# A first layer's last block in two phases: its second product by Strassen's scheme

## The chip, the cores and the metric

The kernel runs on one core of one Trainium2 chip. The metric is the device time of the program in microseconds (us), the median of several executions; lower is better. One execution of each kernel is taken with the hardware profiler, and all views below come from that one. Engines: PE is TensorE (matmuls), DVE is VectorE, ACT is ScalarE, POOL is GpSimd, SP is SyncE. In this kernel SP and POOL mostly issue DMA transfers, each in the order of its own queue: SP mainly loads, POOL mainly stores.

## What is computed

A linear attention with decay, then two MLPs, all in float32 (the weights are drawn in float64 and come to the chip as 64-bit words):

```python
for t in range(S):                                   # 768 steps, 4 batches, 8 heads, D = 64
    state = gamma * state + einsum('bhd,bhe->bhde', k[:, :, t], v[:, :, t])
    y[:, :, t] = scale * einsum('bhd,bhde->bhe', q[:, :, t], state)
x = y.transpose(0, 2, 1, 3).reshape(3072, 512)
h = x @ w_in;   x = np.maximum(0.01 * h, h) @ w_out          # 512 -> 2048 -> 512
h = np.maximum(x @ w_in2, 0.0);   out = (h * h) @ w_out2     # 512 -> 2048 -> 512
```

## The kernel before

**Precision.** Each float32 operand is split into a high and a low part (ACT rounds a copy, DVE subtracts it), and each product is three matmuls: high by high, low by high, high by low. A matmul here has a 128x128 stationary tile and 512 moving columns.

**Blocks.** The 3072 tokens go in three blocks b of 1024. The 2048 hidden rows are 8 pairs q of 128-row tiles. The work on PE stands in this order: block 0 of the first layer, with the attention for it and for block 1 between its matmuls, then blocks 1 and 2 of the first layer, then the three blocks of the second. All matmuls and DMA issues are pinned in the order in which the code is written; on ACT and DVE a scheduler places the rest. Blocks are named (layer, b): (0, 2) is the first layer's last, and the one that is changed.

**First product.** In block 0 it is plain (`emit_plain`). From block 1 on it is a Strassen-Winograd scheme: the 2x2 quarters of the weights and of x give seven products in place of eight. The seven weight sums, split, are tiles `wa` (four units) and `wb` (three), kept in DRAM as `wid`; the seven x sums are made by `operands`.

**Second product, first layer.** Plain in all three blocks. Per block there are two halves of 512 tokens. The first half's matmuls (`put_out`) stand between those of the first product of the following q; the second half (`emit_out` with t = 1) runs after the last q. Each half is 16 tiles of 12 matmuls. The weights are tiles `wo`, loaded from DRAM (`wou`, four raw units for each q) by `read_out`; `make_out` makes them in block 0.

**Second layer, `both_block`.** Two phases. The first is all of the first product, 42 matmuls for each q; its results `gu` and `gt` stay in SBUF. `first_half` does the first four products of q, while `second_half` of q - 1 does its last three, so PE turns to the next q's units after four products. The second phase is the second product as seven Strassen stages of 48 matmuls: `prepare` makes the next stage's g operand (`rot`) during a stage, and the weights `wu` come from `wou` with eight units for each q, four raw and four sums, loaded by `read_stage`.

**Weights.** `cast` makes float32 of float64 words: two passes on ACT, three on DVE. The second layer's `w2` is cast in pieces during the first two blocks (`SOON`; tiles `st` and `sf`, stored as `wflt`). For q in `HERE`, 0 to 4, its second half is loaded and cast in block (0, 2) as one tile `sg` (`units_ahead`), split and summed (`make_units`, `out_units`) and stored to `wou`.

Of the kernel before, what the change touches and what calls it, by code (L numbers as in the profile page):

```python
# [17 lines left out]
P = 128  # L18
# [7 lines left out]
T = 512  # L26
# [17 lines left out]
HERE = (0, 1, 2, 3, 4)  # L44
# [9 lines left out]
def retention_then_two_mlps(  # L54
# [12 lines left out]
    mid = ExitStack()  # L67
    w_p = mid.enter_context(tc.tile_pool(name="w", bufs=1))
# [10 lines left out]
    def swap_pools():  # L79
        early.close()  # L80
        late["ps"] = ctx.enter_context(tc.tile_pool(name="ps_b", bufs=1, space=bass.MemoryType.PSUM))
        late["p"] = mid.enter_context(tc.tile_pool(name="late", bufs=1, reuse_waits="tile"))

    def swap_left():
        mid.close()
        late["p"] = ctx.enter_context(tc.tile_pool(name="units", bufs=1, reuse_waits="tile"))
# [250 lines left out]
    wou = [dram.tile([P, 8 if lay else 4, NQ, 2, 256], F32, name=f"wou{lay}") for lay in range(2)]  # L337
# [16 lines left out]
    def load_piece(n):  # L354
        if n < 2 * len(SOON):
# [40 lines left out]
    def in_tiles(b, q):  # L396
        if b == 1 and q % 2 == 0:
            return [w_p.tile([P, 512 * n], F32R, tag="sg", name=t, bufs=2) for n, t in ((4, "wa"), (3, "wb"))]
        pool = late["p"] if q % 2 and late else w_p
        return [pool.tile([P, 512 * n], F32R, tag=t, name=t, bufs=1) for n, t in ((4, "wa"), (3, "wb"))]  # L400
# [150 lines left out]
    def get_in(b, q):  # L551
        if b == 0:
            plain_in(q)
        else:
            read_wid(0, q, *in_tiles(b, q))

    def make_out(q):
        if q < NQ - 1:
            f = g_p.tile([P, 2, T], F32, tag=f"t{NQ - 1}", name="of", bufs=1).rearrange("p j c -> p (j c)")
        else:  # L560
            f = w_p.tile([P, 1024], F32, tag="wf", name="of", bufs=1)
# [3 lines left out]
        put_wou(q, o)  # L565

    def put_wou(q, o):
        store(
            out=wou[0][:, :, q].rearrange("p n l c -> p n (l c)"),
            in_=o.bitcast(F32).rearrange("p n l c -> p n (l c)"),  # L570
        )
        wout[q] = (o[:, 0:2], o[:, 2:4])

    def out_units(q, n, h, t):
# [4 lines left out]
            out=wou[1][:, n:2 + n, q].rearrange("p n l c -> p n (l c)"),  # L579
# [3 lines left out]
    def make_units(q, f, *to):  # L583

        if q in HERE:
            t = late["p"].tile([P, 1024], U64, tag="sg", name="sg")
            store(out=t, in_=w2[q, 1])
            yield
            cast(t, f)
        else:  # L590
            store(out=f, in_=wflt[q, 1])
        yield
        h = [f[:, n * 512:n * 512 + 512].rearrange("p (n c) -> p n c", n=2) for n in range(2)]
        for n in range(2):
            out_units(q, 2 * n, h[n], to[n])
        yield
# [6 lines left out]
        for n in range(2):  # L603
            out_units(q, 4 + 2 * n, h[n], to[2 + n])

    def scratch(*tags):
        out = []
        for t in tags:
            p = late["r"] if t == "ss" else g_p if t[0] == "t" else late["p"]
# [3 lines left out]
    def read_out(q, spare=None):  # L613
        if spare == "u":
            o = [late["p"].tile([P, 2, 2, 256], F32R, tag=f"u{n}", name="wo", bufs=1) for n in range(2)]
            for n in range(2):
                load(
                    out=o[n].bitcast(F32).rearrange("p n l c -> p n (l c)"),
                    in_=wou[0][:, 2 * n:2 * n + 2, q].rearrange("p n l c -> p n (l c)"),
                )  # L620
        else:
            p, tag, bufs = spare or (o_p, "wo", 2)
            t = p.tile([P, 4, 2, 256], F32R, tag=tag, name="wo", bufs=bufs)
            load(
                out=t.bitcast(F32).rearrange("p n l c -> p n (l c)"),
                in_=wou[0][:, :, q].rearrange("p n l c -> p n (l c)"),
            )
            o = (t[:, 0:2], t[:, 2:4])
        wout[q] = o
# [55 lines left out]
    def act_sbuf(g, on_act):  # L685
        if on_act:
# [99 lines left out]
    def evacuate(b, t):  # L786
        ac = acc.pop((0, b, t))
        for m in range(KB):
            if t:
                if m % 2 == 0:  # L790
# [490 lines left out]
```

## Time and profile before

| | us |
|---|---|
| median of 3 executions | 1108.33 (1108.21 to 1111.32) |
| the profiled execution | 1108.09 |
| its span (first to last instruction) | 1106.3 |
| PE busy | 1094.2 (99% of the span) |
| DVE busy | 703.6 (64%) |
| ACT busy | 582.0 (53%) |
| moved by DMA | 283.87 MB, mean 257 GB/s |

The profile's page gives busy times; its chain of waits follows the work that ended last back through what released it; its tables of stretches give each engine's busy time between two moments. "PEclk" is the clock that the chip granted to PE, 1.00 being full speed. An idle engine costs time only if PE waits for it in the end.

### The profile page before, as it was taken

What the parts mean: (1) busy time and instruction counts of PE and PEld (TensorE: products, weight loads), DVE (VectorE), ACT (ScalarE), POOL (GpSimd) and SP (SyncE); (2) the same over time, 40 slices, a digit from 0 to 9 for tenths busy, and PEclk for the clock granted to TensorE, in tenths of its full rate; (3) what the DMA queues carried; (4) which work ended last, traced back from release to release, by engine and by line L of the source; (5) the groups of instructions that cost most, each with busy time, mean ns of one, the idle gap of its engine ahead of it and who ended that gap; (6) DMA issues with size and microseconds to landing.
All of it is one profiled execution on the core that took longest, in us unless ns stands there. A gap on an engine that the chain in (4) does not pass through costs nothing.

```text
span 1106.3 us, 15285 instructions
## 1 busy us (share of the span) xinstructions
PE 1094.2 (99%) x5647; PEld 869.0 (79%) x5647; DVE 703.6 (64%) x1205; ACT 582.0 (53%) x1052; POOL 77.6 (7%) x134
## 2 busy tenths in 40 slices
PE   9999999999999999999999999999999999999998
PEld 6777777677777777788787788888888888888886
DVE  5867776656666564545448548886655768455853
ACT  5666665444564552355456357655455555455542
POOL 0000000001000000001111112100000001000000
PEclk9999999999999999999999999999999999999999
DMA  9688885867689876599985877989155875357571
GB/s 372 226 307 303 304 312 163 315 199 280 228 300 344 323 225 224 170 347 327 336 322 195 325 255 270 383 284 360 64 177 185 319 250 233 124 194 251 167 244 58
DMA packets 81227, 283.87 MB, mean 257 GB/s; under 512 B 7808, under 2 KB 10368, under 8 KB 72960
## 3 DMA queue, kind: packets, MB, share of 16 engines
q1 hardware_dynamic: 64208, 210.33, 54.8%
q0 software_dynamic: 16800, 72.36, 16.8%
q8 instruction: 45, 0.74, 0.3%
q10 hardware_dynamic: 144, 0.20, 0.1%
q14 instruction: 30, 0.25, 0.1%
HBM read 205.79 MB, written 77.07 MB: 256 GB/s over the span
## 4 chain that ended last, share of the span: by engine, by line
PE 82%; issue 8%; DMA 5%; DVE 3%; POOL 1%; ACT 1%; SPq 0%; POOLq 0%; DVEq 0%; ACTq 0%
PE acc L127 38%; PE pa L127 23%; PE pd L127 8%; PE y L127 5%; PE pb L127 4%; PE sc L127 3%; DMA r<-first 3%; DMA wo<-wou 1%; DMA wflt<-sf 1%; POOL wou L133 1%; PE idle L127 1%; DMA wou<-of 0%; DMA wf<-wraw 0%; DVE gl L763 0%; DVE of L389 0%
## 5 line engine op out<-in xcount | busy, mean ns | idle before, releaser
L127 PE MATMUL acc<-rot,wu 128*128 128x512 f32 x1008 | 235.7, 395 | 0.0
L127 PEld LDWEIGHTS acc<-rot,wu 128*128 128x128 f32 x1008 | 189.2, 188 | 46.0
L127 PE MATMUL pa<-xh,wa 128*128 128x512 f32 x576 | 180.9, 395 | 0.1
L127 PE MATMUL acc<-gh,wo 128*128 128x512 f32 x600 | 160.3, 399 | 3.3 <-DMA wo<-wou 2.5
L127 PEld LDWEIGHTS acc<-gh,wo 128*128 128x128 f32 x600 | 112.4, 190 | 31.5 <-issue 4.6
L127 PEld LDWEIGHTS pa<-xh,wa 128*128 128x128 f32 x576 | 106.1, 188 | 25.4 <-issue 2.2
L127 PE MATMUL pa<-xl,wa 128*128 128x512 f32 x288 | 112.5, 391 | 0.0
L837 ACT CAST rot<-gu 128x512 fp32r<-128x512 f32 x120 | 74.5, 621 | 61.6 <-PE acc L127 54.4
L838 DVE TENSOR_TENSOR rot<-gu,rot 128x512 fp32r<-128x512 f32 x120 | 82.1, 689 | 38.5 <-ACT rot L837 38.0
L127 PE MATMUL pd<-xh,wa 128*128 128x512 f32 x320 | 99.2, 390 | 1.3 <-DVE wa L485 0.7
L127 PE MATMUL pa<-xh,wb 128*128 128x512 f32 x320 | 99.8, 393 | 0.0
L127 PE MATMUL acc<-gl,wo 128*128 128x512 f32 x300 | 85.4, 392 | 0.0
L763 DVE TENSOR_TENSOR gl<-g,gh 128x512 fp32r<-128x512 f32 x75 | 50.6, 687 | 35.0 <-ACT gh L762 20.1
L127 PEld LDWEIGHTS pd<-xh,wa 128*128 128x128 f32 x320 | 60.0, 188 | 15.2 <-DVE wa L485 1.4
L127 PEld LDWEIGHTS pa<-xh,wb 128*128 128x128 f32 x320 | 59.5, 188 | 12.9
L127 PEld LDWEIGHTS acc<-gl,wo 128*128 128x128 f32 x300 | 56.3, 188 | 12.9 <-DVE gl L763 0.3
L127 PEld LDWEIGHTS pa<-xl,wa 128*128 128x128 f32 x288 | 54.1, 188 | 11.6
L127 PE MATMUL acc<-gg,wo 128*128 128x512 f32 x252 | 62.9, 398 | 0.0
L127 PE MATMUL pa<-xl,wb 128*128 128x512 f32 x160 | 62.4, 390 | 0.0
L127 PE MATMUL pd<-xl,wa 128*128 128x512 f32 x160 | 62.4, 390 | 0.0
L127 PEld LDWEIGHTS acc<-gg,wo 128*128 128x128 f32 x252 | 46.8, 188 | 11.9 <-issue 1.4
L687 ACT ACTIVATE gt<-gt 128x512 f32<-128x512 f32 x48 | 30.4, 633 | 46.6 <-DVE gt L856 32.5
(141 smaller groups left out, 1628.3 us busy)
## 6 DMA issues: line engine op xcount, KB each, us to landing
wu<-wou SPq DMA_DIRECT2D x84, 512.0 KB, 5.5
wo<-wou SPq DMA_DIRECT2D x32, 1024.0 KB, 8.2
wa<-wid SPq DMA_DIRECT2D x28, 1024.0 KB, 7.4
wb<-wid SPq DMA_DIRECT2D x28, 768.0 KB, 5.3
sg<-w SPq DMA_DIRECT2D x16, 1024.0 KB, 7.4
wou<-of POOLq DMA_DIRECT2D x32, 512.0 KB, 5.8
r<-first SPq DMA_DIRECT2D x50, 256.0 KB, 6.9
wid<-wa POOLq DMA_DIRECT2D x12, 1024.0 KB, 7.1
```

Of the source, the lines that this page charges most:

```text
L127: pin(nc.tensor.matmul(**kw))
L133: pin(nc.gpsimd.dma_start(**io))
L687: nc.scalar.activation(out=g, in_=g, func=AF.Relu)
L763: mark[1] = seq(nc.vector.tensor_tensor(out=gl, in0=g, in1=gh.bitcast(F32), op=ALU.subtract)).ins
L837: mark[0] = nc.scalar.copy(r[:, 0], s).ins
L838: mark[1] = nc.vector.tensor_tensor(out=r[:, 1], in0=s, in1=r[:, 0].bitcast(F32), op=ALU.subtract).ins
```

## The change

- Block (0, 2) is run by `both_block` as well, with `lay` 0: first product for all q, then the second product in seven stages.
- `wou` of the first layer gets eight units for each q. The four sums are made and stored in block 0 by `out_sums`, behind `make_out` of the next q.
- `HERE` is 0 to 3. Their units are made in the first phase of (0, 2) by `units_inline`, which loads the float64 words in two halves `st` from POOL's queue; q = 4 is cast in block (0, 1) by `last_pieces`, and its units are made in the second phase.
- `gu` tiles lie where weight tiles lay (`kept`); the pools are swapped in block (0, 1), not after (0, 2). The load of `xs` for (1, 0) moves from the first product of (0, 2) into its fourth stage; `units_here` of q = 0 and 1 moves into the second phase.
- `make_in(1, 0)` and its loads move from the end of block 0's first half into its second half.

```diff
-HERE = (0, 1, 2, 3, 4)
+HERE = (0, 1, 2, 3)
...
-    wou = [dram.tile([P, 8 if lay else 4, NQ, 2, 256], F32, name=f"wou{lay}") for lay in range(2)]
+    wou = [dram.tile([P, 8, NQ, 2, 256], F32, name=f"wou{lay}") for lay in range(2)]
...
+    def out_sums(q):
+
+        with aside():
+            to = [x_p.tile([P, 2 * T], F32, tag=t, name="of") for t in ("xh4", "xl4")]
+            sum_units(0, q, stage.pop(("of", q)), *to)
...
+    def units_inline():
+
+        def get(q):
+            kinds = ((late["r"], "ss", 2), (w_p, "wf" if q < 2 else "wb", 1))
+            t = [p.tile([P, 512], U64, tag=tag, name="st", bufs=n) for p, tag, n in kinds]
+            for n in range(2):
+                store(out=t[n], in_=w2[q, 1][:, 512 * n:512 * n + 512])
+            return t
+
+        st = get(HERE[0])
+        yield
+        to = quarters()
+        for q in HERE:
+            f = late["r"].tile([P, 1024], F32, tag="ss", name="of", bufs=2)
+            for n in range(2):
+                cast(st[n], f[:, 512 * n:512 * n + 512])
+            if q + 1 in HERE:
+                st = get(q + 1)
+            yield
+            yield from all_units(q, f, *to)
+            yield
+        f = x_p.tile([P, 1024], F32, tag="xl4", name="of")
+        yield from make_units(HERE[-1] + 1, f, *to)
...
+    def kept(q):
+
+        if q in (5, 7):
+            return w_p.tile([P, 2, T], F32, tag="wf" if q == 5 else "wb", name="gu", bufs=1)
+        if q not in ahead:
+            t = w_p.tile([P, 2, 2, T], F32, tag="wa" if q == 4 else "sg", name="gu", bufs=1 if q == 4 else 2)
+            ahead[q], ahead[6 if q == 4 else q + 1] = t[:, 0], t[:, 1]
+        return ahead.pop(q)
...
+                if lay == 0 and n and (k == 1 or k == 3 and n in (1, 2, 4, 5)):
+                    with aside():
+                        next(here, None)
...
+        at = {4: (7, 13), 5: (5, 11), 6: (1, 5, 9)} if lay else {4: (13,), 5: (5, 11), 6: (1, 4, 8, 12)}
...
-                    if n == 1 and not last:
-                        read_x(b + 1)
-                    if n in (3, 5) and not last:
-                        read_units((n - 3) // 2)
...
+                    if n == (1 if lay else 3) and nl is not None:
+                        read_x(nb)
+                    if n in (3, 5) and lay and nl is not None:
+                        read_units(1, (n - 3) // 2)
+                if lay == 0:
+                    if (n, e) in ((0, 1), (0, 9), (0, 15)):
+                        with aside():
+                            next(here, None)
+                    if (n, e) in ((1, 1), (2, 13)):
+                        made = units_here(n - 1, x_p.tile([P, 1024], F32, tag="xh4", name="of"))
+                        next(made)
...
+                    if q:
+                        plain_in(q + 1)
+                        for n in (q - 1,) if q < 5 else (4, 5) if q == 5 else (6,):
+                            out_sums(n)
...
+            if b == 0 and i in (2, 11):
+                load_in(i // 11)
+            elif b == 0 and i == 6:
+                with aside():
+                    for _ in make_in(1, 0):
+                        pass
...
+            elif b == 1 and i == 12:
+                swap_left()
+                swap_right()
+                here = units_inline()
+                next(here)
+                read_units(0, 1)
...
+    for lay, b in ((0, NB - 1), (1, 0), (1, 1), (1, 2)):
+        both_block(lay, b, here)
```

Where the instructions stand is shown at three places. The first is DVE in a q-step of block 0, the step that the timeline of the rows below shows (`pm` and `s` belong to the attention, `wf` is the next q's first weights, `sf` a piece of `w2`, `of` the second weights of the first layer). Before:

```order
L388 TENSOR_SCALAR wf<-wf 128x1024
L389 SCALAR_TENSOR_TENSOR wf<-sg,wf 128x1024
L763 TENSOR_TENSOR gl<-g,gh 128x512
L392 ISA wf<-sg,wf 128x2048
L233 TENSOR_TENSOR pm<-sc,tab_79 128x256 x2
L241 SCALAR_TENSOR_TENSOR s_1394<-state,tab_78,sc 128x64
L388 TENSOR_SCALAR sf<-sf 128x512
L389 SCALAR_TENSOR_TENSOR sf<-st,sf 128x512
L392 ISA sf<-st,sf 128x1024
L419 TENSOR_TENSOR wa<-wf,wa 128x1024
```

The same step of the changed kernel:

```order
L578 TENSOR_TENSOR of<-of 128x256
L384 SCALAR_TENSOR_TENSOR wf<-sg,wf 128x1024
L579 TENSOR_TENSOR of<-of 128x256
L387 ISA wf<-sg,wf 128x2048
L580 TENSOR_TENSOR of<-of 128x256
L228 TENSOR_TENSOR pm<-sc,tab_79 128x256 x2
L236 SCALAR_TENSOR_TENSOR s_1430<-state,tab_78,sc 128x64
L383 TENSOR_SCALAR sf<-sf 128x512
L581 TENSOR_TENSOR of<-of 128x256
L384 SCALAR_TENSOR_TENSOR sf<-st,sf 128x512
L387 ISA sf<-st,sf 128x1024
L413 TENSOR_TENSOR wa<-wf,wa 128x1024
```

Four additions (`of<-of 128x256`) came in: two inside the conversion of `wf`, one behind it, one between `pm` and `wa`.

The second is ACT in the first product of (0, 2). Before, `g` rows bring PE's results out, and the cast of a whole `sg` tile stands in one place between two q:

```order
L720 ACTIVATE g<-pa 128x512
L762 CAST gh<-g 128x512 x2
L386 ACTIVATE of<-sg 128x1024
L387 ACTIVATE sg<-sg 128x1024
L682 COPY g<-pa 128x512
L682 COPY g<-pd 128x512
L576 CAST of<-of 128x2x256 x2
L682 COPY g<-pa 128x512
```

In the changed kernel, `gu` and `gt` rows bring the results out; this is the place at which the halves `st` of q = 1 are cast:

```order
L693 ACTIVATE gu<-gu 128x512
L868 COPY gt<-pa 128x512
L843 CAST rot<-gu 128x512
L382 ACTIVATE st<-st 128x512
L895 ACTIVATE gu<-pa 128x512
L568 CAST of<-of 128x2x256
L382 ACTIVATE st<-st 128x512
L693 ACTIVATE gt<-gt 128x512
L862 COPY gu<-pa 128x512
L381 ACTIVATE of<-st 128x512 x2
```

The two `st<-st` rows, each the first to read a loaded half, stand ahead of `gt` and `gu` rows that bring out PE's results.

The third is the queue of SP at the turn from block (0, 1) to (0, 2) (`wid_7_98<-ma` and `mc` are stores of made weights; `wid_1_84` holds the units of q = 1). Before:

```order
L130 DMA wo<-wou_123 128x4x512
L130 DMA wid_7_98<-ma 128x1024
L130 DMA wid_7_98<-mc 128x768
L130 DMA wo<-wou_123 128x4x512
L130 DMA wa<-wid_1_84 128x2048
L130 DMA wb<-wid_1_84 128x1536
L130 DMA wo<-wou_123 128x4x512
L130 DMA wa<-wid_2_85 128x2048
L130 DMA wb<-wid_2_85 128x1536
```

In the changed kernel:

```order
L125 DMA wo<-wou_123 128x4x512
L125 DMA wid_7_98<-ma 128x1024
L125 DMA wid_7_98<-mc 128x768
L125 DMA wa<-wid_1_84 128x2048
L125 DMA wb<-wid_1_84 128x1536
L125 DMA wa<-wid_2_85 128x2048
L125 DMA wb<-wid_2_85 128x1536
```

The loads of `wo` between those of `wa` and `wb` are gone, so each load of units follows on the one before.

## Rows read from the trace of the kernel before

**Rows 1.** The page, busy time, share of the span and instructions of each engine.

```profile
PE 1094.2 (99%) x5647; PEld 869.0 (79%) x5647; DVE 703.6 (64%) x1205; ACT 582.0 (53%) x1052; POOL 77.6 (7%) x134
```

**Rows 2.** Stretches of three blocks: us; PE, PEld, DVE, ACT, POOL busy (x); PEclk; DMA; GB/s.

```profile
467.21:638.71 171.50, 168.29 (x722) 135.83 (x721) 93.77 (x142) 84.66 (x137) 24.50 (x40) 0.99 0.84 304
638.71:793.31 154.60, 154.60 (x674) 126.16 (x673) 117.21 (x186) 91.27 (x154) 18.56 (x31) 1.00 0.76 280
793.31:947.92 154.61, 154.61 (x674) 126.15 (x673) 100.15 (x146) 81.05 (x134) 4.32 (x8) 1.00 0.61 218
```

**Rows 3.** Chain of waits from the old block's last wait on: start us, us, what.

```profile
596.60 12.47 DMA wo<-wou
609.20 29.52 PE acc L127 x120
...
714.90 78.41 PE acc L127 x336
```

**Rows 4.** Stretches behind the `wo` wait and at a second-layer phase's end; columns as rows 2.

```profile
605.00:610.00 5.00, 2.49 (x10) 1.78 (x9) 3.43 (x4) 1.54 (x3) 0.65 (x2) 0.90 1.04 411
610.00:615.00 5.00, 5.00 (x18) 3.93 (x18) 1.92 (x2) 0.81 (x2) 0.42 (x1) 0.76 1.04 406
701.30:714.90 13.60, 13.60 (x61) 11.26 (x61) 12.43 (x22) 8.95 (x16) 2.88 (x4) 1.00 1.02 419
```

**Rows 5.** Groups on DVE, shapes apart: shape, xcount, busy us, mean ns, idle before.

```profile
L233 DVE TENSOR_TENSOR pm<-sc,tab 128x256 f32<-128x256 f32 x64 | 25.4, 419 | 8.6 <-PE sc L127 5.0 <-PE y L127 3.4
L577 DVE TENSOR_TENSOR of<-of 128x512 fp32r<-128x512 f32 x32 | 21.4, 687 | 4.7 <-ACT of L576 4.6
...
L392 DVE CUSTOM_DVE_ANT_0 sf<-st,sf 128x1024 uint16<-128x1024 uint16 x22 | 15.2, 689 | 1.3 <-ACT g L720 0.5
```

**Rows 6.** Groups on ACT, shapes apart, columns as rows 5.

```profile
L576 ACT CAST of<-of 128x512 fp32r<-128x512 f32 x32 | 18.9, 619 | 9.1 <-DVE of L600 3.4 <-DVE of L392 2.8 <-DMA of<-wflt 2.3
...
L387 ACT ACTIVATE st<-st 128x512 uint32<-128x512 uint32 x22 | 14.7, 670 | 0.0
```

**Rows 7.** Stretches of block 0, first and second half; columns as rows 2.

```profile
40.00:165.00 125.00, 124.95 (x707) 97.88 (x706) 91.95 (x139) 80.54 (x126) 9.00 (x14) 1.00 0.81 290
165.00:260.00 95.00, 93.07 (x608) 71.15 (x607) 61.48 (x116) 45.76 (x87) 4.75 (x9) 1.00 0.68 220
```

**Rows 8.** Chain of waits in block 0, one piece in two successive q-steps; columns as rows 3.

```profile
117.08 5.48 PE pa L127 x24
...
136.20 5.48 PE pa L127 x24
```

**Rows 9.** Timeline of DVE in a q-step of block 0: start us, us, instruction, idle before.

```profile
121.38 1.22 DVE L392 CUSTOM_DVE_ANT_0 wf<-sg,wf 128x2048 uint16<-128x2048 uint16 x1
123.52 0.76 DVE L233 TENSOR_TENSOR pm<-sc,tab 128x256 f32<-128x256 f32 x2 [0.93 <-PE sc L127]
...
128.02 1.23 DVE L419 TENSOR_TENSOR wa<-wf,wa 128x1024 fp32r<-128x1024 f32 x1 [1.67 <-ACT wa L418]
```

**Rows 10.** Timeline of ACT in the same q-step, columns as rows 9.

```profile
126.95 1.04 ACT L418 CAST wa<-wf 128x1024 fp32r<-128x1024 f32 x1
```

**Rows 11.** Timeline of PE at the same q-step's end, columns as rows 9.

```profile
130.41 0.73 PE L127 MATMUL pa<-xh,wa 128*128 128x512 f32 x2
```

**Rows 12.** Timeline of SyncE's DMA queue ahead of the old block, columns as rows 9.

```profile
464.26 0.74 SPq L130 DMA_DIRECT2D wo<-wou  x1
465.05 1.04 SPq L130 DMA_DIRECT2D wa<-wid  x1
```

**Rows 13.** Tile `wa`, loads issued from 463 to 475 by SyncE.

```profile
DMA to landing us min/median/max: 11.4/13.0/14.7
```

**Rows 14.** Tile `sg`, the five loads issued by GpSimd (old block, 1024 KB each).

```profile
DMA to landing us min/median/max: 7.3/14.2/15.5
```

**Rows 15.** DMA issues, 467 to 639, then 639 to 795: KB each, median us to landing.

```profile
wa<-wid SPq DMA_DIRECT2D x6, 1024.0 KB, 10.9
...
wa<-wid SPq DMA_DIRECT2D x6, 1024.0 KB, 7.2
```

More of the change, by code (lines that the diff above doesn't have):

```diff
@@ L578, in out_units, with sum_units @@
         store(
-            out=wou[1][:, n:2 + n, q].rearrange("p n l c -> p n (l c)"),
+            out=wou[lay][:, n:2 + n, q].rearrange("p n l c -> p n (l c)"),
             in_=t.rearrange("p (n c) -> p n c", n=2),
         )
[L583 to L596, printed above, removed]
+    def sum_units(lay, q, f, *to):
         a11, a21, a12, a22 = (f[:, n * 256:n * 256 + 256] for n in range(4))
@@ L613, in read_out @@
     def read_out(q, spare=None):
[L614 to L629, printed above, removed]
+        p, tag, bufs = spare or (o_p, "wo", 2)
+        t = p.tile([P, 4, 2, 256], F32R, tag=tag, name="wo", bufs=bufs)
+        load(
+            out=t.bitcast(F32).rearrange("p n l c -> p n (l c)"),
+            in_=wou[0][:, 0:4, q].rearrange("p n l c -> p n (l c)"),
+        )
+        wout[q] = (t[:, 0:2], t[:, 2:4])
     xop = {}
@@ L979, in both_block @@
                 for m in range(2):
-                    put = load if last and i == 4 else store
-                    put(out=out[b][:, 2 * mh + m, t * T:(t + 1) * T], in_=y[:, m])
+                    put = load if nl is None and i == 4 else store
+                    put(out=(out if lay else ydr)[b][:, 2 * mh + m, t * T:(t + 1) * T], in_=y[:, m])
     start = ExitStack()
@@ L1074, in side, with last_pieces @@
             next_half()
-    def units_ahead(q):
-        f = late["p"].tile([P, 1024], F32, tag="of", name="of", bufs=2)
-        to = [w_p.tile([P, 2, 1024], F32, tag="sg", name="of", bufs=2) for _ in range(2)]
-        g = make_units(q, f, *(t[:, n] for t in to for n in range(2)))
-        next(g)
-        return g
+    def last_pieces(i):
+        n = EARLY + NQ
+        q, half, _ = piece(n)
+        if i == 0:
+            stage["last"] = [x_p.tile([P, 512], U64, tag=t, name="st") for t in ("xh7", "xh3")]
+            for k in range(2):
+                load(out=stage["last"][k], in_=w2[q, half][:, 512 * k:512 * k + 512])
+        elif i == 4:
+            f = stage["f"] = x_p.tile([P, 1024], F32, tag="xl7", name="sf")
+            with aside():
+                for k in range(2):
+                    cast(stage["last"][k], f[:, 512 * k:512 * k + 512])
+        elif i == 7:
+            load(out=wflt[q, half], in_=stage["f"])
     def split_late(i):
@@ L1085, in split_late @@
         halves[j] = split_g(g1.pop(j), f"t{LATE[i // 2 - 1]}" if i % 2 and i > 1 else None)
-    for b in range(NB):
-        nl, nb = (0, b + 1) if b + 1 < NB else (1, 0)
-        rest = (b + 2) * B * NP if b + 1 < NB else 0
+    ahead = {}
+    for b in range(NB - 1):
+        rest = (b + 2) * B * NP
         for q in range(NQ):
-            ahead = 0 < q < NQ - 1
+            more = 0 < q < NQ - 1
             if b == 0:
@@ L1107, in retention_then_two_mlps @@
                 emit_plain(q, 1, 1)
-                if ahead:
+                if more:
                     put_out(b, 2 * q - 1)
@@ L1125, in retention_then_two_mlps @@
                     next(new, None)
-                if b == 1:
-                    side(2 * q)
-                elif 0 < q < 6 and q - 1 in HERE:
-                    with aside():
-                        next(made)
-                if ahead:
+                side(2 * q)
+                if more:
                     put_out(b, 2 * q - 1, (6, 12))
```

207 lines of the change are left out of this document (91 added, 116 removed).

## The prediction

> **What bounds the kernel now.** I read the page first: TensorE (PE) is busy 1094.2 us of a span of 1106.3 [rows 1]. So nothing matters but the number of matmuls, the pace at which they go, and new holes between them. Then I split the span at the block borders with the table of stretches [rows 2]. The block that is changed (first layer, last block; I call its start S) runs from 467.21 to 638.71: 171.50 us, of which PE is busy 168.29. The next two rows are blocks of the second layer, which already have the form that the changed block gets: 154.60 and 154.61 us with PE busy for all of it. The chain of waits gives the pace [rows 3]: 336 matmuls of a second phase take 78.41 us, 0.2334 each; the first phase, from 638.71 to 714.90, takes 76.19 for its 336. The same view shows why the old block is looser than its 720 matmuls: it waits for a load of `wo` until 609.20, and the 120 matmuls behind it take 29.52 us, 0.246 each. [...] At 0.2334 the 120 would have taken 28.0, so the hole cost 2.5 + 1.5 = 4.0 us.
>
> **What the change takes away.** The new block has 336 + 336 matmuls for 336 + 384: 48 x 0.2334 = 11.2 us (10.9 to 11.8 at 0.227 and 0.246 each). Its second phase reads `wu` in the order of the second-layer blocks and has no `wo` loads, so the hole of 4.0 goes as well. The whole step from 171.50 to 154.60 is 16.9; what the two terms leave (1.7) is looseness at the turn between the halves and the slower start. I take 16.9 as the gain of a block that nothing holds up, and put every hold-up against it.
>
> **Block 0: sums.** `out_sums` adds to each of eight q-steps four additions of 128x256 and two splits of 128x512. On DVE that is 4 x 0.419 + 2 x 0.687 = 3.05 us, on ACT 2 x 0.619 = 1.24 [rows 5, 6]. A q-step is 136.20 - 117.08 = 19.12 us [rows 8], and DVE is busy 91.95 of 125 there [rows 7], 14.1 a step. With the sums it is 17.1, 90%. The cover is real: in the q-step that the trace shows, DVE stands idle for 0.93 us before `pm` and for 1.67 before `wa` [rows 9], and the order puts two additions inside the conversion of `wf`, one behind it and one between `pm` and `wa`. The three ahead of `pm` (1.26 us) cost nothing: ACT comes to the cast of `wa` only at 126.95 [rows 10], 4.35 us after DVE ended `wf` at 122.60. The one behind `pm` is taken up by the 1.67, and the `wa` subtraction, which ends at 129.25, has 1.2 us more until PE wants it at 130.41 [rows 11]. Only the step that carries two sums (`out_sums` of 4 and 5 at q = 5: 14.1 + 6.1 = 20.2 us in 19.1) overruns, by about 1 us. I take 1.0; the bounds are 0 (idle time takes all) and 4 (half a microsecond in each step).
> The stores of the sums are 8 x 1.05 MB. Seven fall into the 125 us, where 36.25 MB were moved (290 GB/s): 43.6 MB, 349 GB/s. At 701.3 to 714.9 the trace has 419 GB/s for 13.6 us with PE never idle [rows 4], so 349 fits, with longer landings. I put nothing on it and keep it in the rival below.
> [...]
>
> **Turn of block 0 and of block 1.** `make_in(1, 0)` goes from the end of block 0's first half into its second. PE is idle for 1.93 us in the 95 us after 165, against 0.05 in the 125 before [rows 7], so the move can give or take 1 to 2; I put 0.5 as a cost. At S the units of q = 1 are new on the path: a product takes 76.19 / 56 = 1.36 us, the old block wanted them after seven products, at S + 9.5, the new one, which turns to q = 1 after four, at S + 5.4 = 472.65. In SyncE's queue they stand behind two stores of `wid` as before, but no longer behind `wo`. The old load was issued at 465.05, 0.8 behind a `wo`, and took at least 11.4 us [rows 12, 13]; at the 7.2 of a second-layer block [rows 15], where no `wo` runs beside it, and issued 0.8 earlier, it lands at 471.5. With 11.4 it lands at 475.7 and costs 3.0. I take 0.5.
>
> **First phase of the new block.** This is the costliest unknown. `units_inline` makes the second layer's units for q = 0 to 3: for each q two float64 halves loaded by GpSimd, converted (ACT 4 x 0.670; DVE 2 x 3 passes of up to 0.689), four splits and four additions. On DVE that is some 8.2 us for each q in two steps of 9.52 us (76.19 / 8). Over the block DVE comes to: 100.15 of a second-layer block without side work, less 16 squarings of 0.69 (the first layer has a leaky ReLU, on ACT), plus 4 x 8.2, plus 4.4 for the units of q = 4, plus some 8 for two sets of first-product units: 134 of 154.6 us, 87%. The block at 638.71 has 117.21 of 154.60 without a hole [rows 2], so 134 is beyond what the trace shows to be free.
> Nearer is the queue of ACT. The cast of the second `st` half of q = 1 stands ahead of the `gt` and `gu` rows that free PE's accumulators (the order of ACT above). Laid on the grid of 9.52 us, that load can be issued at about S + 20.7, when the tile before it has been read, ACT comes to it at S + 25.7, and PE feels it 1.5 us later: 6.5 us for the landing. A q's two halves are together one old `sg` load, which from GpSimd's queue landed after 7.3 to 15.5, median 14.2 [rows 14]. So the price is 0.8 at 7.3 and 7.7 at 14.2, and up to three q have it. The old `sg` ran beside 1.05 MB of `wo` in each step that the new block doesn't load; scaled as `wa` is between the two kinds of block (7.2 to 10.9 [rows 15]) 14.2 becomes 9.4: 2.9 us once. The loads of q = 2 and 3 have more room, and the tightly packed steps behind them less than 1 us: I put 0.6 on these. Together 3.5, between 0 and 12. The traffic is 6.82 MB in 19.04 us (two sets of first units 3.67, float64 1.05, stores 2.10): 358 GB/s.
>
> **Second phase.** Only splits of `rot` and the units of q = 4 run there; a `rot` is wanted a stage (78.41 / 7 = 11.2 us) after it can be made. The load of `xs` now stands in SyncE's queue ahead of the last eight `wu` loads and waits for the last `wou` store, which the third stage issues (by S + 110); those `wu` are wanted from the sixth stage on, S + 76.2 + 5 x 11.2 = S + 132. I put nothing on it. The two second-layer blocks that follow are as before.
>
> **Sum** against the profiled execution's own 1108.09 us (span 1106.3; 0.24 under the median 1108.33): 1108.1 - 16.9 + 1.0 + 0.5 + 0.5 + 3.5 = 1096.7.
>
> **Rivals.** (a) Nothing is held up: 1108.1 - 16.9 = 1091.2, with half a microsecond in block 0. For it: the block at 638.71 has 77% of DVE and 419 GB/s in places and not one hole. Against: the queue of ACT behind `st`.
> (b) The first phase is bound by its loads. If they move no faster than the old block's 304 GB/s [rows 2], 6.82 MB take 22.4 us for 19.04, 3.4 more; over the 3.5 pairs of steps that is 11.8, and with the small terms 1108.1 - 16.9 + 2.0 + 11.8 = 1105.0. For it: `sg` landed after 14.2. Against: 419.
> (c) Slower than before: block 0 becomes DVE's. DVE takes its instructions in order; if the idle time before `pm`, `wa` and the rest (5.0 us a step) can't be used because what DVE waits for moves along with it, each sum adds its 3.05: 8 x 3.05 = 24.4, so 1108.1 - 16.9 + 24.4 + 5 = 1120.6. It decides from 16.9 / 8 = 2.1 us a step on, less with (b)'s costs. Against: most additions stand ahead of the waits, not behind.
> (d) The change doesn't do all it says: the dense pace doesn't come, and only the 48 matmuls are saved. 1108.1 - 11.2 + 6.0 = 1102.9.
>
> **How the numbers follow.** A measurement of this kernel tells 0.3% (3.3 us) from no change. Forecast (1093 to 1101) 0.58; (a), 1090.5 to 1093, 0.10; (b), 1101 to 1109, 0.17, half of it over 1104.8; (c) 0.09; (d) 0.06. Faster by over 0.3%: 0.58 + 0.10 + 0.08 + 0.06 = 0.82; within 0.3%: 0.10; slower: 0.08. The range leaves out most of (c) and the upper half of (b): 1090.5 to 1105.
>
> **What will show it.** PE matmuls `acc<-rot,wu` x1344, and the block from S to the next in 155 to 160 us. Waits of PE for ACT in the first phase, with ACT waiting for `st`, show the 3.5; none would make (a). In block 0 a q-step of 19.1 us, 20 in the one with two sums; over 21 in each makes (c). If waits of PE for `wa` at S or for `wu` in the second phase come to several microseconds, my handover or my reading of SyncE's queue was wrong.

## The result, and the profile after

The changed kernel takes 1098.28 us in the median of five executions (1097.05 to 1103.25), the kernel before 1108.33 (1106.28 to 1111.32): a ratio of 0.9912, 95% interval 0.9886 to 0.9939. Forecast were 1096.7 and a range of 1090.5 to 1105. The sum came out to 1.6 us; several of its terms did not, as the profile shows. The profiled execution took 1098.28, span 1096.5, so 9.8 less than the 1106.3 before. The page, busy time by engine:

```profile
PE 1082.8 (99%) x5599; PEld 859.4 (78%) x5599; DVE 761.5 (69%) x1327; ACT 609.2 (56%) x1105; POOL 91.8 (8%) x154
```

48 matmuls fewer and 11.4 us less of PE; DVE has 58 us more. The stretches of the changed block's two phases and of the first phase of (1, 0), to hold against [rows 2], with the same columns:

```profile
470.15:548.19 78.04, 76.77 (x337) 62.91 (x337) 57.12 (x102) 52.79 (x94) 15.34 (x24) 1.00 0.93 353
548.19:626.60 78.41, 78.41 (x337) 63.07 (x337) 66.94 (x107) 44.86 (x74) 7.34 (x12) 1.00 0.70 261
626.60:705.01 78.41, 77.04 (x338) 62.83 (x337) 59.56 (x105) 51.98 (x92) 17.80 (x29) 1.00 0.88 322
```

The changed block takes 78.04 + 78.41 = 156.45 us where it took 171.50: 15.05 less. Its second phase has the pace of [rows 3] to the hundredth; that of (1, 0) takes 78.42. But the first phase of (1, 0), 76.19 before, is now 78.41: 2.2 us lost in a block that the prediction left as it was. Waits of PE over the whole span (what waited, what for: us in total, times, longest):

```profile
PE pa L122 <- DMA wa<-wid: 2.1, 3, 1.0
PE pa L122 <- ACT g L749: 1.9, 2, 1.6
PE idle L122 <- DVE zero L1025: 1.5, 1, 1.5
PE pa L122 <- DVE wa L413: 1.2, 1, 1.2
PE pd L122 <- DVE wa L479: 0.8, 1, 0.8
PE pa L122 <- ACT wa L412: 0.8, 1, 0.8
PE acc L122 <- DVE wo L413: 0.7, 1, 0.7
PE pa L122 <- DVE gt L878: 0.5, 1, 0.5
```

The waits with `g`, `wa` L412/L413 and `wo` lie in block 0. From the chain of waits, with the start of the last q of block 0's first half (the 24 `pa` matmuls of q = 7) and of the blocks:

| | q = 7 | (0, 1) | (0, 2) | its second phase | (1, 0) | (1, 1) | span |
|---|---|---|---|---|---|---|---|
| before | 174.26 | 260.13 | 467.21 | | 638.71 | 793.31 | 1106.3 |
| changed | 181.89 | 264.64 | 470.15 | 548.19 | 626.60 | 783.43 | 1096.5 |
| difference | +7.63 | +4.51 | +2.94 | | -12.11 | -9.88 | -9.8 |

So: block 0's first half +7.6; its second half -3.1; block (0, 1) -1.6; the changed block -15.05; (1, 0) +2.2; nothing behind it. Losses of 9.9 stand against gains of 19.7, and the experiments ask for the causes, but for the 1.6 of block (0, 1). In the kernel before PE waits 0.69 us there, at 415.44 for the attention's `s`, in the changed one it doesn't; whether that explains the 1.6 was not tested, and two runs below whose edits leave this block alone gain only 0.4 and 0.5 in it.

### The profile page after: what moved, and what is told of

Read it like the earlier page. It is cut to its first block, busy times and chain, and to the rows that moved or that the text cites. A ratio compares the mean times of both kernels' runs of the same rounds, so it can differ in the third digit from the quotient of the medians.

```text
span 1096.5 us, 15509 instructions
## 1 busy us (share of the span) xinstructions
PE 1082.8 (99%) x5599; PEld 859.4 (78%) x5599; DVE 761.5 (69%) x1327; ACT 609.2 (56%) x1105; POOL 91.8 (8%) x154
## 4 chain that ended last, share of the span: by engine, by line
PE 91%; DMA 5%; DVE 2%; ACT 1%; issue 1%; SPq 0%; DVEq 0%; ACTq 0%
PE acc L122 44%; PE pa L122 24%; PE pd L122 9%; PE y L122 5%; PE pb L122 4%; PE sc L122 3%; DMA wa<-wid 3%; DMA sg<-w 2%; DMA r<-first 1%; PE idle L122 1%; ACT sg L382 0%; SPq L125 0%; ACT g L749 0%; ACT of L568 0%; DVE wf L439 0%
## 5 line engine op out<-in xcount | busy, mean ns | idle before, releaser
L122 PE MATMUL acc<-rot,wu 128*128 128x512 f32 x1344 | 314.3, 395 | 0.0
L122 PEld LDWEIGHTS acc<-rot,wu 128*128 128x128 f32 x1344 | 252.3, 188 | 61.3
L843 ACT CAST rot<-gu 128x512 fp32r<-128x512 f32 x160 | 99.3, 620 | 79.5 <-PE acc L122 68.8
L844 DVE TENSOR_TENSOR rot<-gu,rot 128x512 fp32r<-128x512 f32 x160 | 109.3, 689 | 47.3 <-ACT rot L843 46.5
L122 PE MATMUL acc<-gh,wo 128*128 128x512 f32 x400 | 106.0, 397 | 0.7 <-DVE wo L413 0.7
L122 PEld LDWEIGHTS acc<-gh,wo 128*128 128x128 f32 x400 | 74.0, 188 | 19.3 <-issue 1.5
L844 DVE TENSOR_TENSOR rot<-gt,rot 128x512 fp32r<-128x512 f32 x64 | 44.1, 691 | 30.9 <-ACT rot L843 30.5
L843 ACT CAST rot<-gt 128x512 fp32r<-128x512 f32 x64 | 39.5, 621 | 38.2 <-PE acc L122 35.4
L122 PE MATMUL acc<-gl,wo 128*128 128x512 f32 x200 | 56.8, 391 | 0.0
L883 DVE TENSOR_TENSOR gu<-gu,pb 128x512 f32<-128x512 f32 x32 | 22.0, 687 | 42.1 <-PE pb L122 42.1
```

The source lines that it names most:

```text
L122: pin(nc.tensor.matmul(**kw))
L843: mark[0] = nc.scalar.copy(r[:, 0], s).ins
L844: mark[1] = nc.vector.tensor_tensor(out=r[:, 1], in0=s, in1=r[:, 0].bitcast(F32), op=ALU.subtract).ins
L883: nc.vector.tensor_tensor(out=u[:, 0], in0=u[:, 0], in1=pb, op=ALU.add)
```

## The experiments

Losses of block 0 below are the start of q = 7 in the one profiled execution of a run, against 174.26. The runs of the kernel before that stood beside these had medians of 1106.39 to 1110.64, so medians are compared through ratios to them.

### The changed kernel again

> The changed kernel once more, unedited, beside the next one on the same chip: 1097 to 1101 us; the first product of q = 7 in block 0 at 181 to 186 us (174.3 before the change), since two other kernels with the same block 0 gave 181.6 and 185.4.

Measured: 1100.31 us (1096.24 to 1101.3), ratio 0.9909 (0.9887 to 0.993), span 1094.5. Block 0 loses 5.86 this time, (1, 0) 77.42 + 78.41. Kernels with the same rows in block 0, run below for other reasons, lose 7.4 and 11.1. The loss is there each time, but its size is not a constant of the program: what follows on block 0 rests on which holes a profile shows, and on sizes only beyond that spread, or where several runs agree.

### The first phase: are stores of the units what delays `wa`?

In the changed block PE waits for a load once, for `wa` of the first product, and never for ACT; ACT waits for `st` once, 0.6 us. The timeline of PE, the wait in brackets:

```profile
504.95 0.73 PE L122 MATMUL pa<-xh,wa 128*128 128x512 f32 x2 [0.77 <-DMA wa<-wid]
```

and the chain of waits, the load ahead of it and the end of the phase:

```profile
494.69 10.22 DMA wa<-wid
...
545.79 0.69 DVE gt L878
546.49 0.04 issue
546.53 1.66 PE pa L122 x6
```

The load is issued when a buffer comes free and took 10.22 us, at 353 GB/s over the phase, 387 and 428 in the pieces 500 to 505 and 505 to 510. This run leaves out the stores of the units made in the first phase, and of those of q = 4 (other units are read in their place), and keeps all work on ACT and DVE:

```diff
-        store(
-            out=wou[lay][:, n:2 + n, q].rearrange("p n l c -> p n (l c)"),
+        if lay == 0 or q > 4:
+            store(
+                out=wou[lay][:, n:2 + n, q].rearrange("p n l c -> p n (l c)"),
```

> The units of w2 for q = 0 to 4 are made in (0, 2) but not stored; the second layer's stages read the first layer's units for these q (output not the reference's). In the first phase of (0, 2), 78.04 us in the changed kernel where 76.19 is dense, this takes away 2.1 of 6.8 MB in each pair of q-steps. Theory: the loss of 1.85 comes from the load of wa for q = 4, which had 9.8 us to land and took 10.2 among these stores: the first phase goes to 76.2 to 76.6 with no wait for wa, (0, 2) to 154.6 to 155.0 us. Rival A (the order of ACT and DVE, full with conversions, holds PE up): all that work is still there, so the first phase stays at 77.5 to 78.5.

Measured: 1097.36 us, ratio 0.9906 (0.9884 to 0.9927). The stretches of the two phases:

```profile
470.93:547.90 76.97, 76.48 (x337) 62.99 (x337) 56.93 (x102) 53.24 (x94) 4.45 (x9) 1.00 0.77 275
547.90:626.30 78.40, 78.40 (x337) 63.08 (x337) 67.92 (x108) 45.79 (x75) 5.43 (x11) 1.00 0.59 214
```

At 275 GB/s instead of 353, with ACT and DVE as busy, the wait for `wa` is gone and the phase takes 76.97, a little more than the 76.2 to 76.6 expected. So of the 1.85 us above 76.19 in the changed kernel 1.1 are due to the stores, and 0.8 are left, of which 0.5 are a wait of PE for `gt` at the end of the phase, where an addition for the next units comes before the last product; this wait stands in every variant. The eleven profiled executions that have the stores take 77.38 to 78.69 for the phase, so the stores' part is 0.4 to 1.7.

### Block (1, 0): a store at the head of POOL's queue

PE waits there at 642.60 (0.99) and 672.08 (0.38) for `wa`, whose loads the chain of waits has at 10.44 and 9.82 us, against a median of 7.2 before [rows 15]. POOL's timeline (DMA issues; idle time before one in brackets):

```profile
630.63 0.54 POOL L128 DMA_DIRECT2D wid<-wa  x1 [31.62 <-DVE wa L479]
631.16 0.54 POOL L128 DMA_DIRECT2D wid<-wb  x1
631.69 3.21 POOL L128 DMA_DIRECT2D ydr<-ss  x6
636.45 0.54 POOL L128 DMA_DIRECT2D of<-wflt  x1 [1.55 <-DVE gt L878]
```

The store of the units of q = 1 stood at the head of POOL's queue for 31.62 us, until DVE had made them; six stores of `ydr` stood behind it and all went out when (1, 0) had begun and was loading its `wa`. This run makes the second step of those units later, so that four of the six stores of `ydr` stand ahead:

```diff
-                    if n in (2, 4) and e in (3, 9):
+                    if (n, e) in ((2, 3), (2, 9), (4, 3), (6, 9)):
```

> The second step of the units of q = 1 (their last splits and their stores to wid) is issued in the seventh stage of (0, 2), not in the fifth, so that in POOL's queue four stores of ydr come ahead of these stores. Nothing is left out. In the changed kernel POOL stood for 31.6 us at the store of wid, and six stores of ydr with two of wid and three loads went out together at 630 to 647, where the first load of wa of (1, 0) took 10.4 us and was waited for. Theory: spread out, the traffic at the start of (1, 0) falls by 1 MB, the first wa lands in under 9.8 us, and (1, 0) goes from 156.8 to 154.6 to 155.7 us. Rival: the wait comes from the loads and stores of (1, 0)'s own units, which are all still there: 156 to 157 us.

Measured: (1, 0) from 630.79 to 786.22, 155.43 us for 156.83; the chain has one load of `wa` left there where it had two:

```profile
636.29 9.84 DMA wa<-wid
...
707.81 78.41 PE acc L122 x336
```

That is within the 154.6 to 155.7 expected, but hardly beyond the spread. The first phase of (1, 0) takes 77.42 to 78.70 in the eight executions that have the early step and the second layer's stores, and 77.02, 76.82 and 77.45 in the three with the late one; the third of these, in the last run below, has 155.86 for the block and misses the expectation. So the place of the store is worth some 0.9 us on average (77.96 to 77.10), and what makes the rest of the 2.2 was not shown. The time is 1097.9, ratio 0.9913 (0.9888 to 0.9939), no better than the changed kernel: in this execution block 0, with the same rows, lost 11.1.

### The turn of block 0: the kernel before with `make_in(1, 0)` moved alone

```diff
-            elif b == 0:
-                load_in(0)
-                for _ in make_in(1, 0):
-                    pass
-                load_in(1)
...
+            if b == 0 and i in (2, 11):
+                load_in(i // 11)
+            elif b == 0 and i == 6:
+                with aside():
+                    for _ in make_in(1, 0):
+                        pass
```

> The kernel before with one part of the change alone: make_in(1, 0) and its loads moved from the end of block 0's first half into its second. In the changed kernel the stretch from q = 7's first product to the start of (0, 1) is 3.0 us shorter than before, with no wait of PE in it (before: 0.3, 0.8 and 0.8 us). Theory: the move itself gives this, so that this kernel is 2 to 3.5 us faster than before, with block (0, 1) starting at 256.6 to 258. Rival: the changed kernel gains there because block 0 is late and its loads have had more time; then the move alone gives 0 to 1.

Measured: 1106.45 us, ratio 0.9978 (0.9962 to 0.9994). The second half of block 0, as in [rows 7]:

```profile
165.00:260.00 95.00, 94.91 (x619) 73.30 (x618) 62.46 (x117) 46.54 (x88) 6.49 (x12) 1.00 0.70 229
```

PE's idle time of 1.93 us is 0.09, and (0, 1) starts at 257.34 for 260.13: 2.8 us earlier. That is the 3.1 of the changed kernel to within 0.3, so the move alone gives nearly all of it.

### Block 0: the sums' stores, the sums' work, or where they stand

Three runs take the stores and the work away. The first leaves out the eight stores of sums (`if lay:` ahead of the store in `out_units`; raw units are read in place of sums), and the scheduler then orders ACT and DVE differently:

> The sums of block 0 are made but not stored (no store of 16 x 512 KB); the stages of (0, 2) read the raw units in their place, so the output is not the reference's. Measure: the start of the attention piece (sc) of q = 7, 179.84 us before the change and 187.31 after it, a loss of 7.5 in block 0's first half. Theory T (the transfers of the sums lengthen the landings of sg, and ACT stands waiting for them): the loss falls to 0 to 2, sc at 180 to 182, ACT's wait for sg back to about 3 us from 6.2, and the program 4 to 7 us shorter than the changed kernel. Rival D (DVE has too much to do): the DVE work is all there, so the loss stays at 6 to 7.5 and the program's time with it.

Measured: 1098.15 us, ratio 0.9915 (0.9882 to 0.9949), loss 5.3, with 265 GB/s from 40 to 172 us for 315. That is between what either theory expected, and PE still waits 1.95 us for `g`, at 126.89. So the order is a variable of its own. In the next two it is held: the rows of ACT and DVE stand as in the changed kernel. One stores an eighth of each sum (`[:, :, 0:64]` of 512 columns), the other stores a sixteenth and also adds and splits only 32 of 256 columns:

```diff
+        c, e = (256, 512) if lay else (32, 32)
-        nc.scalar.copy(u[:, :, 0], h)
+        nc.scalar.copy(u[:, :, 0, 0:c], h[:, :, 0:c])
```

> The changed kernel with ACT and DVE held to its own order of instructions, row for row, and each store of block 0's sums cut to an eighth of its columns (the stages of (0, 2) read the raw units in place of the sums, so the output isn't the reference's). Only the transfers of the sums are gone, 7 of 8 MB. The loss up to q = 7's first product in block 0 is 7.5 us in the changed kernel (7.2 and 11.0 in the two other kernels with the same block 0), and 5.2 where the stores were left out but the scheduler set another order. Theory T (transfers lengthen the landings of sg): 0 to 2.5. Rival D (work of the sums on DVE and ACT): 5 to 8. Rival O (the order of instructions itself is worse, whatever their length): 5 to 11.

Measured: 1095.62 us, ratio 0.9885 (0.9868 to 0.9902), loss 3.95.

> As the run with small stores and small sums, but the small stores read the tiles of the sums, so that ACT no longer waits until a store has read the float32 weights (2.7 us of ACT's waiting there, and 21.4 in the run with large stores from these weights, which therefore says nothing on the sums). Held to the changed kernel's order on ACT and DVE. First product of q = 7 in block 0: small stores alone gave 178.2 us (174.3 before the change). Rival D (the work of the sums): 174.3 to 175.5. Theory O (the order in which the work stands): 176.5 to 178.2, with the wait for wo in the second q-step and the one for wa in the step of two sums still there.

Measured: 1094.76 us, ratio 0.9864 (0.9837 to 0.9891), loss 3.65. From the changed kernel to the first, nearly all of the stores' bytes are gone and the loss is 1.9 to 7.2 less, and the ratios fall from 0.9912 and 0.9909 to 0.9885. From the first to the second, most of DVE's added work is gone too (DVE is busy for 110.31 and 99.15 of the 132 us from 40 to 172, before for 95.80) and the loss is 0.3 less. So without the stores DVE's amount of work, which the prediction priced, is worth about 0.3, by one execution each. What it is worth beside the stores is not shown. Some 3.7 are left, with the order as in the changed kernel. In the second run the waits of PE are these, at the two places where the order differs from before:

```profile
58.54 0.50 PE L202 MATMUL acc<-gh,wo 128*128 128x512 f32 x1 [0.82 <-DVE wo L493]
```
```profile
153.24 0.50 PE L202 MATMUL pa<-xh,wa 128*128 128x512 f32 x1 [1.15 <-DVE wa L493]
```

Place A is the second q-step: `of` now has two buffers, so ACT converts the next `of` ahead of the cast of `wo`. Place B is the step with two sums. ACT's timeline there in the changed kernel:

```profile
149.63 1.13 ACT L568 CAST of<-of 128x512 fp32r<-128x512 f32 x2
150.66 1.16 ACT L382 ACTIVATE sg<-sg 128x1024 uint32<-128x1024 uint32 x1
151.70 0.67 ACT L381 ACTIVATE sf<-st 128x512 f32<-128x512 f32 x1
152.26 0.70 ACT L382 ACTIVATE st<-st 128x512 uint32<-128x512 uint32 x1
152.85 1.04 ACT L412 CAST wa<-wf 128x1024 fp32r<-128x1024 f32 x1
```

`wf` was done at 149.65 by DVE's timeline; the cast of `wa` comes behind two casts of sums and three conversions, 3.2 us later, and PE waits 0.78 and 1.21 us there. ACT runs its rows one behind the other here, at 149.63, 150.66, 151.70, 152.26 and 152.85. On DVE the same shows at 125.41: it stands idle for 1.39 us until ACT's `wf` is there, with the first addition of the sums behind it, which runs only at 126.02, though its `of` was last split at 105.66.

The starts of PE's pieces against those of the kernel before (36.93 for the first 12 `pa` matmuls after the start, then the x24 rows at 59.74, 136.20, 155.31 and 174.26) show where each loss arises, in us:

| | ahead of A | at A | A to B | at B | behind B | loss |
|---|---|---|---|---|---|---|
| changed | 0.50 | 1.01 | 2.06 | 3.90 | 0.16 | 7.63 |
| changed again | 1.18 | 0.90 | 0.99 | 2.55 | 0.24 | 5.86 |
| unstored units of the first phase | 0.71 | 1.02 | 1.39 | 4.09 | 0.15 | 7.36 |
| late step in (1, 0) | 0.94 | 0.89 | 1.54 | 7.57 | 0.17 | 11.11 |
| an eighth of the sums stored | 0.52 | 0.99 | 0.00 | 2.27 | 0.17 | 3.95 |
| a sixteenth stored, small sums | 0.52 | 1.08 | 0.40 | 1.49 | 0.16 | 3.65 |

The first four have the same block 0. A costs 1 us in every row. The 1 to 2 us between A and B and part of those at B come with the stores, and the spread between equal programs is nearly all at B.

The stores' part shows in the chain of waits of the changed kernel, at the longer of PE's other two waits of block 0:

```profile
114.34 9.83 DMA sg<-w
...
125.29 1.14 ACT sg L382
126.42 0.48 ACT g L749
126.91 0.04 issue
126.95 3.04 PE pa L122 x12
```

The stretch from 40 to 172 us of the changed kernel, columns as [rows 2] (285 GB/s in the kernel before):

```profile
40.00:172.00 132.00, 127.35 (x707) 98.76 (x706) 108.75 (x179) 86.53 (x137) 17.89 (x26) 0.99 0.87 315
```

`sg`, the next weights in float64, lands late; ACT waits for it (1.49 us at 124.25) with the `g` that frees PE's accumulator queued behind. Two things make it late. The load goes out at 114.34, where it went out at 110.02 before, and in the two held runs at 114.15 and 114.18: that comes with the order. And it takes 9.83 us; in the two held runs ACT doesn't wait for this load, nor PE for `g` anywhere in block 0's first half: that comes with the stores. Landings of `sg` from 40 to 172 us (min/median/max), first in the kernel before, then changed, then with a sixteenth stored:

```profile
DMA to landing us min/median/max: 4.8/6.1/13.2
```
```profile
DMA to landing us min/median/max: 4.7/7.3/15.0
```
```profile
DMA to landing us min/median/max: 4.8/6.2/15.6
```

Three more runs were to separate stores from work by storing the unsummed float32 weights `of`. One, with sums left out:

> Block 0 stores the float32 weights twice where the sums were stored (16 x 512 KB as before), but makes no sums: no additions, no splits (the output is not the reference's). Theory T: the loss of 7.5 us up to sc of q = 7 stays at 5 to 7.5. Rival D: it falls to 0 to 2. If both kernels lose about half, the loss needs both: late sg and a DVE without idle time to catch up.

Measured: 1117.18 us, ratio 1.0089 (1.0065 to 1.0113), loss 19.2. Two, in the held order, with additions and splits of 32 columns, storing all of `of`, then 64 columns of it:

> The changed kernel, held to its order, with the additions and splits of block 0's sums done on an eighth of their columns; the stores have their full size, from the float32 weights (output not the reference's). DVE is relieved of some 1.5 to 2 of the 3.05 us that the sums add to a q-step (what stays is the start of each instruction). Theory T: loss 5 to 8 us. Rival D: 0 to 3. Rival O: 5 to 11.

Measured: 1107.37 us, ratio 0.9988 (0.9976 to 1.0), loss 16.6. That a part of each instruction's time stays was an estimate from [rows 5]: 0.419 us for 256 columns, 0.687 for 512.

> Both at once, held to the same order: small stores and small sums (output not the reference's). Under T and under D the loss in block 0 is gone: 0 to 1.5 us, and the start of (0, 1) at 256 to 258 us, since the second half of block 0 gains 3 in the changed kernel. Under O it stays at 5 or more. If p6 and p7 each keep 3 to 5 and this keeps 0 to 1.5, both shares count.

Measured: 1095.9 us, ratio 0.9875 (0.986 to 0.9889), loss 3.95. They don't tell the theories apart. In the last two a store that reads `of` holds its buffer, and ACT's next conversion waits for it, 2.7 us in the run of 1095.9. In the run of 1107.37, ACT's longest wait from 40 to 172 us:

```profile
ACT of L461 <- DMA wou<-of: 21.4, 5, 6.0
```

That wait is the experiments' own; the changed kernel stores from the split sums instead. In the run of 1117.18 it is only 1.4 us, and the cause of its loss was not followed up.

### Does the order mend block 0?

First, three orders set by hand and all else left to the scheduler: the cast of `wo` ahead of the next `of`, that of `wa` ahead of the two sums, and the later step in (1, 0).

```diff
-        cast(stage.pop((q, 1)), f, 1 if q else 2)
+        with behind_both(stage["wo"]) if q else ExitStack():
+            cast(stage.pop((q, 1)), f, 1 if q else 2)
...
-                            out_sums(n)
+                            with behind_both(stage["wa"]) if n == 5 else ExitStack():
+                                out_sums(n)
```

> The changed kernel with nothing left out and three places put in another order. First, the float64 conversion of a q's second weights in block 0 is issued behind the split of the q before (wo), as the one buffer of before forced it. Second, the sums of q = 5 are issued behind the split of the first weights of q = 6 (wa). Third, the second step of q = 1's units in (0, 2) goes to the seventh stage, as in the earlier run. If the order of ACT and DVE costs what the trace shows at these places (1.5 us at the second q-step of block 0, 2.3 with the slow matmuls behind it in the step with two sums, 1.4 at the start of (1, 0)), the program is 4 to 5 us shorter than the changed kernel: 1093 to 1095. Rival: in block 0 what counts is the amount of work and traffic in each step, and the delay only moves to the next wait (wo for wa); then 1 to 2 us, from the third place alone: 1096 to 1098.

Measured: 1101.3 us (1097.98 to 1102.91), ratio 0.9923 (0.9902 to 0.9944). Place A is mended (the x24 row of the second q-step starts at 59.80; 59.74 in the kernel before, 61.25 in the changed one) and (1, 0) is 155.24, but the loss at q = 7 is 10.7: the scheduler moved other rows. At B the cast of `wa` now stands ahead of the sums' casts, yet ACT comes late to it, and PE waits 2.63 and 0.95 us for `wa`. So a last run holds all rows as in the changed kernel up to block (0, 1) and moves only two splits, of `wo` at A and of `wa` at B; it has the later step in (1, 0) too. As a difference of ACT's rows (DVE's splits move along):

```diff
+CAST wo<-of 128x4x256
 ACTIVATE of<-sg 128x1024
 ACTIVATE sg<-sg 128x1024
-CAST wo<-of 128x4x256
...
+CAST wa<-wf 128x1024
 CAST of<-of 128x2x256 x2
 ACTIVATE sg<-sg 128x1024
 ACTIVATE sf<-st 128x512
 ACTIVATE st<-st 128x512
-CAST wa<-wf 128x1024
```

> The changed kernel with ACT and DVE held in its own order up to block (0, 1), but for two splits: that of wo in the second q-step stands ahead of the conversion of the next of, and that of wa in the step with two sums ahead of the two casts of sums and of the conversions of the last of and sf. The second step for units of q = 1 in (1, 0) is made at the seventh stage and later. Nothing is left out.
> Theory (part of block 0's loss comes from where these two splits stand, part from the sums' store traffic): PE takes up the x24 row of the second q-step at 59.7 to 59.9 us instead of 61.25 and has no wait for wa in the step with two sums; the block's first half then loses 3.5 to 5.5 us against the kernel before instead of 7.5, what is left being waits for sg; block (1, 0) takes 154.6 to 155.7. The time falls by 3 to 5.5 us against the changed kernel, to 1093 to 1096.
> Rival (as with the three hand-set orders: what is gained at a place is lost behind it, since the sg loads and ACT set the pace): the x24 row comes at 59.8 but the last q of the first half starts no earlier than 181, and the time is 1097 to 1100.

Measured: 1100.14 us (1097.68 to 1101.77), ratio 0.9934 (0.9915 to 0.9952). The rival was right. Both places are mended: the x24 row comes at 60.16 (0.4 late, as its first 12 `pa` matmuls already were), and `wa` is there in time at B. But the loss at q = 7 is 8.3, nearly all of it from one hole behind B, in the chain of waits:

```profile
148.66 1.13 ACT of L593 x2
149.79 1.06 ACT sg L407
150.85 0.57 ACT sf L406
...
152.47 11.33 DMA sg<-w
...
166.53 0.51 ACT g L774
167.04 0.04 issue
167.08 5.49 PE pa L147 x12
```

SyncE's queue brings the load of `sg` out behind a store of `sf` and loads of `st` and `r`, so it goes when ACT and DVE are through with the last `sf`: at 152.47, 15.4 us behind the x24 row of its q-step at 137.06. In the kernel before it went at 147.31, 11.1 behind that at 136.20 [rows 8]; in the changed kernel 13.5 behind. Then it takes 11.33 us, with 421 GB/s in the piece from 160 to 165, and PE waits 4.51 us for `g`. That removing the sums' rows from ahead of `sf` would bring the load out in time was not tried. No version with all its work in it beat the changed kernel by more than the intervals.

## Why the prediction was right, and where its steps failed

- **The dense block, -16.9.** Right: its second phase has 78.41 us, and without the stores of units the block came to 155.37. In the 4.0 us put on the old block's hole, the 2.5 are PE's idle time from 605 to 610, and the 1.5 go with a granted clock of 0.90 and 0.76 in that stretch and the next [rows 4]. Rival (d) is out by this, rival (a) by the hold-ups found.
- **Sums in block 0, +1.0 with 4 as the upper bound.** Mis-sized, and this is the step that failed: 5.9 to 11.1 in the executions of the same rows, 0.5 to 1.2 of it ahead of A. The step with two sums, for which 20 us were forecast, took 21.7 to 26.7. The premise held as far as it was tested (the idle time of DVE takes the amount of work, all but about 0.3 by the pair of held orders, without the stores). Three things were missed: ACT's order at A, caused by the second `of` buffer; at B a cast of `wa` queued behind the casts of the sums, where the prediction counted DVE's time alone; and "I put nothing on it" for the stores. 315 GB/s over 132 us did fit, but the landings of `sg` got longer and its loads later, and the `g` that PE wants stood behind them on ACT. Rival (c) named the right block and priced it at 24.4 by DVE's work alone: DVE is busy 108.75 of those 132 us, and taking most of the sums' work from it, once the stores were gone, gave 0.3.
- **Turn of block 0, +0.5.** The sign was wrong: -2.8, shown by the move alone. The sentence that it "can give or take 1 to 2" left the sign open, but the size is beyond it. Part of block 0's loss was so paid back, and another 1.6 in block (0, 1), whose cause was not tested.
- **Handover at S, +0.5.** No wait of PE for `wa` stands there: 0.
- **First phase, +3.5.** Half the size, 1.85, and not by the mechanism given. ACT hardly waited for `st`, whose halves landed in 5.6 us in the median (9.4 had been scaled from old loads for the two together); PE waited 0.77 us for a `wa` that took 10.22 us to land. That is the place of rival (b) at about a tenth of its price (1.1 for 11.8). Stores of units made it, as the run without them shows.
- **Second phase, 0.** Right.
- **"The two second-layer blocks that follow are as before".** Wrong for the first, +2.2 (77.42 in the first phase of the repeat, so +1.2 there). Units moved into the second phase left their store at the head of POOL's queue, which accounts for some 0.9 of it; the rest is open. The queue of SyncE was followed past each moved step, that of POOL was not.

In sum the forecast had the main term right, the 16.9 of the dense block. That it met 1098.28 to 1.6 us is in good part luck, because terms missed on both sides: 6.6 more in block 0, 2.2 in (1, 0), against 3.6 less at the turn, 1.6 in (0, 1), 1.7 in the first phase and 0.5 at S; the block itself agrees with its row.

On traffic: with one core at work, 428 GB/s stand for 5 us; but the waits for landings appeared at means of 315 and 353, below that.

## What to carry to other kernels

Where work is added between the steps of a full pipeline, price it not by the idle time of the engine but by the rows that come to stand behind it: a cast that PE wants (here 3.2 us behind the tile that it reads), a conversion that frees a buffer, a load queued behind that conversion's store (15.4 us into its q-step where it went at 11.1). A moved store counts on its own queue too: one that waited for late work held back the six stores behind it, here for 31.62 us, and let them go when the next block was loading its own weights. In the two runs that mended single places of such an order nothing was gained (ratios 0.9923 and 0.9934 for 0.9912): the next late load or cast opened holes that cost as much again (10.7 and 8.3 us at q = 7 for 7.63).

## What the runs showed of the hardware

Behind waits of 2.0 us PE was granted 0.66 of its clock over 5 us in one execution, behind waits of 2.2 us 1.00 in another. The stretches of the changed kernel at B, columns as [rows 2]:

```profile
150.00:155.00 5.00, 3.66 (x30) 2.32 (x28) 4.57 (x8) 5.00 (x8) 1.92 (x3) 1.00 0.82 244
155.00:160.00 5.00, 4.34 (x12) 3.43 (x13) 4.69 (x7) 1.27 (x3) 0.00 (x0) 0.66 0.94 345
```

the second of them in the repeat of the changed kernel, with 2.2 us of waits at B:

```profile
155.00:160.00 5.00, 4.66 (x20) 3.82 (x21) 4.20 (x7) 1.10 (x2) 0.00 (x0) 1.00 0.97 376
```

and the run with two moved rows behind its hole:

```profile
165.00:170.00 5.00, 2.92 (x7) 2.34 (x8) 4.90 (x9) 3.77 (x6) 2.12 (x3) 0.61 0.72 289
170.00:175.00 5.00, 5.00 (x18) 3.95 (x17) 2.16 (x3) 2.40 (x3) 0.03 (x1) 0.70 0.99 361
```

In the changed kernel waits of 2.0 us were followed by 5 us at a granted 0.66, and the 11 `pa` matmuls behind them took 4.38 us; in the repeat waits of 2.2 us, of the same rows, cost no clock, and the same 11 took 2.81. With stores and work cut, 1.15 us at B cost none either: the stretch from 155 to 160 was granted 1.00. The wait of 4.5 us in the last run was followed by 0.61 and 0.70, and the 12 `pa` matmuls behind it took 5.49 us where the same piece a little later takes 2.94.

So at B the same rows lost 2.55 us for 2.2 us of waits with the clock at 1.00, 3.90 and 4.09 for 2.0 and 2.2 us of waits with 4.38 and 4.03 us for the 11 matmuls behind them, and 7.57 for 4.5 us of waits with 5.06 us for those 11: between 1.2 and 2 times the length of the hole. The slower matmuls make some 1.5 us of the spread between 5.9 and 11.1 (4.09 against 2.55, for equal waits). Why the clock fell in one execution and not in the other, and why the waits were twice as long in one, stays open.
